# Uneven output products in one block, earlier weights' products, and another order at the start of batch 1, in a Fourier-mixing and gated-MLP kernel

## The chip, the cores and the metric

The kernel runs on one core of a Trainium2 chip. The metric is the device time of one execution in microseconds (us), lower is better. The core has five engines that run side by side and wait for each other through semaphores: TensorE (PE in the profile) multiplies matrices, VectorE (DVE), ScalarE (ACT) and GpSimd (POOL) work element by element, and SyncE (SP) issues most of the transfers. Each engine takes its instructions in the order in which the program lists them.

## The reference

The input `x` has 8 batches of 3008 rows of 256 numbers. It is Fourier transformed over the rows and over the columns, the real part is kept, and every row of the result goes through a gated two-layer network.

```python
X = np.fft.fft(x, axis=1)
X = np.fft.fft(X, axis=2)
x = X.real.reshape(B * S, D)                  # (24064, 256)
gate = np.maximum(x @ w_gate, 0.0)            # w_gate, w_val: 256 x 1536
val = x @ w_val
out = (gate * val) @ w_out                    # w_out: 1536 x 256
```

## The kernel before

The transform over the 256 columns is multiplied into the weights: `WA` and `WB` (index 0 for the gate, 1 for the value) are products of small cosine and sine tables `TA`, `TB` with the loaded weights, made in thirds of 512 columns by `weights` (L420). The first third is made at the start; `weights(1)` and `weights(2)` each give four steps, and each step is two matmuls into a bank of the pool `psO`, and a copy into `WA` or `WB` by ScalarE or VectorE.

The transform over the rows is made by matmuls with tables `tabC`, `tabS` (L585 in the profile). For each batch it gives `U` and `V`, with 1505 positions each. One position stands for two output rows that mirror each other: the first row's gate is a sum of products with `WA` and `WB`, and the other row's is reached by adding one more product with the negative doubled sine part (`mirror`, L880). The same holds for the value.

Batch 0 is worked in four blocks (`segments`) of 376 or 377 positions, the other batches in three blocks (`thirds`). A block has 12 tiles, one for each 128 of the 1536 hidden columns. In batch 0 a tile (`single_tile`, or `first_tile` in the first block) runs so: gate product of the first rows (two matmuls), relu on ScalarE into `r`; the mirror product of the tile before into its value bank `v`, and that tile's second `h` on VectorE; value product of this tile (two matmuls), first `h` (L899); a few output products; extra steps; mirror product into this tile's gate bank, second relu; a few more output products. The output products (L781, 256 columns each, `o<-wo,h`) belong to the block before, whose `h` are complete: they wait as a list, `todo_out`, from which `run` takes the next few. Two units of 128 rows share a bank of `psO`, and after 24 products a copy `os<-o` by ScalarE (L794) is put on the list `evict`. `run` ends with `flush`, which issues the copies on the lists, as long as tiles are not paired (that is in batch 0). Steps of the next batch's transform come from the list `todo_dft`, at counts given in tables such as `DFT_0`.

The third block is `blk == 2`. The second block's output products begin early, in its own last four tiles (24 of 72), so that 48 are left for the third block: `per_tile` is 4, and each tile took 2 and 2.

The dictionary `more` holds the extra steps by block and tile. In the first block there stand the eight steps of the weights (tiles 0 to 7), then the steps of the even tables; at tile 2 of the third block stands `gate_128`: it makes `b2`, 128 x 12 numbers, by turning row 0 of `WB[0]` with twelve matmuls of one column, and VectorE copies them out of the bank (L836, L837). `b2` is needed from batch 1 on.

From batch 1 on the order is that of `slot`. A tile's gate is split: `sine_part` makes the product with `V` in the only bank of `psG` (L1015), and ScalarE copies it out (L1018); `seed` has ScalarE write a scaled row `CB` times `b2` into a bank of `psP` (L1010), and `cosine_part` adds the product with `U` there (L1022); `both` forms the two gates on VectorE and GpSimd (L1026, L1027). While one tile (`cur`) is at its value product, the sine and cosine parts of the tile after next (`nxt`) are made, and the one behind that is seeded. The first tile of batch 1 has `lead` set. The last tile of batch 0 makes the first two tiles' parts in its steps `last`.

Of the kernel before, what the change touches and what calls it, by code (L numbers as in the profile page):

```python
# [11 lines left out]
F32 = mybir.dt.float32  # L12
# [17 lines left out]
def dram(ap, offset, pattern):  # L30
    return bass.AP(ap.tensor, offset, [list(p) for p in pattern])
# [3 lines left out]
def kernel(  # L35
# [27 lines left out]
    def single(name, shape, dt=F32, pool=const):  # L63
        return pool.tile(shape, dt, name=name, tag=name)
# [438 lines left out]
    start_pool.__exit__(None, None, None)  # L503
    ch128 = nc.dram_tensor("ch128", (B, 4 * NJ + 1), BF16, kind="Internal").ap()
    b2 = single("b2", [128, NF])
    one = single("one", [1, 1], BF16)
    nc.vector.memset(one[:], 1.0)


    def even_table(n, c):  # L510
# [311 lines left out]
    fold_even()  # L822
    turns_and_rows()

    more = {(0, i): [s] for i, s in enumerate(weights(1) + weights(2))}
    for n, c in enumerate(even_order):
        for k, step in enumerate(even_table(n, c)):
            more.setdefault(divmod(EVEN_AT[n] + k, NF), []).append(step)
# [1 line left out]
    for seg in (2, 3):  # L830
        more.setdefault((1, 8 + seg), []).append(lambda seg=seg: minus_v(nc.scalar, seg))

    def gate_128():
        p = psD.tile([128, 512], F32, name="d", tag="d")
        for f in range(NF):
            nc.tensor.matmul(p[:, f:f + 1], lhsT=WB[0][0:1, f * 128:(f + 1) * 128], rhs=one[:], start=True, stop=True)  # L836
        nc.vector.tensor_scalar(b2[:], p[:, 0:NF], scalar1=1.0, op0=ALU.mult, scalar2=None)  # L837
    more[(2, 2)] = [gate_128]
    more_1 = {}
    for at, step in zip((-5, -4, -3, -2, -1, 7, 7, 8, 14, 17), channel_loads() + channel_turn()):  # L840
        (more_1 if at >= 0 else more).setdefault(at if at >= 0 else (3, NF + at), []).append(step)

    DFT_0 = (0, 0, 0, 0, 0, 3, 0, 0, 4, 3, 3, 0), (0, 0, 0, 0, 0) + (1,) * 7, (3, 3, 3, 3, 3, 3, 0, 0, 0, 0, 0, 0)

    DFT_EVEN = (3, 0, 3, 0, 0, 0) * 4 + (0,) * 12
    DFT_1 = (3, 0, 3, 0, 0, 0) * 4 + (0, 1, 0, 1, 1) + (0,) * 7
# [4 lines left out]
    def run(todo, n):  # L851
        for _ in range(min(n, len(todo))):
            todo.pop(0)()
        if not paired:
            flush()
# [84 lines left out]
    def single_tile(st, outs, extra=(), last=(), tag="p"):  # L940

        gate(st, tag)
        if pending is not None:
            finish(pending)
        value(st)
        mult(st, 0)
        run(todo_out, outs)
        for step in extra:
            step()
        mirror(st["g"], st, 0)  # L950
        relu(st)
        run(todo_out, outs)
        for step in last:
            step()
        return st

    def first_tile(st, extra, outs):
# [47 lines left out]
    def seed(st, p=None):  # L1005

        if st is None or st["kind"] == "o":
            return
        st["p"] = p or bank("p")
        nc.scalar.activation(st["p"][:, 0:st["n"]], st["c"], ACTF.Copy, scale=b2[:, st["fi"]:st["fi"] + 1])  # L1010
# [18 lines left out]
    def slot(cur, mid, nxt, after, outs, fold_us):  # L1029

        stop = len(todo_out)

        def out(part):
            run(todo_out, len(todo_out) - stop + outs * part // 8)
        old = nxt is not None and nxt["kind"] == "o"
        new = nxt is not None and not old
        if old:
            gate(nxt)
        lead = cur["lead"]
        if lead:  # L1040
            out(5)
        if new and mid["kind"] != "o":
            sine_part(nxt)
        out(3 if not lead else 5)
        out(5)
        if new and mid["kind"] == "o":
            sine_part(nxt)
        if new:
            cosine_part(nxt)
        seed(after)  # L1050
        if pending is not None:
            mirror(pending["v"], pending, 1)
        if pending is not None:
            second(pending)
        value(cur)
        if cur["kind"] == "o":
            mult(cur, 0, cur["first"])
        else:
            relu_mult(cur, 0)
        if new:  # L1060
            both(nxt)
        if old:
            nxt["first"] = nxt["r"]
            mirror(nxt["g"], nxt, 0)
            relu(nxt)
        run_fold(fold_us)
        run_one(evict)
        run_one(sums)
        out(8)
        return cur  # L1070
# [4 lines left out]
    for b in range(B):  # L1075
# [4 lines left out]
        for blk, block in enumerate(blocks):  # L1080
# [53 lines left out]
            elif not paired:  # L1134
                for fi in range(NF):
                    st = tile_of(block, fi, (U, V, CB))
                    add_h(st, hs)
                    tag = {(3, 8): "g", (3, 9): "d", (3, 10): "g", (3, 11): "d"}.get((blk, fi), "p")
                    last = []
                    if (blk, fi) == (3, 11):  # L1140
                        last = [lambda: (sine_part(ahead[1]), cosine_part(ahead[1]), both(ahead[1]), seed(ahead[2]))]
                    if (blk, fi) == (3, 9):
                        ahead = [next(tiles) for _ in range(3)]
                        more[(3, 9)] += [lambda: seed(ahead[0], prime())]
                        more[(3, 10)] += [lambda: seed(ahead[1], prime())]
                        more[(3, 11)] += [lambda: (sine_part(ahead[0]), cosine_part(ahead[0]), both(ahead[0]))]
                    if (blk, fi) == (1, 8):
                        run(todo_out, len(todo_out))
                        todo_out = out_steps(b, block, hs, True)
                    pending = single_tile(st, 3 if blk == 1 else per_tile // 2, more_b.get((blk, fi), ()), last, tag)  # L1150
                    run(todo_dft, DFT_0[blk - 1][fi])
            else:
                for fi in range(NF):
# [59 lines left out]
```

## Time and profile before

| | |
|---|---|
| median of 3 runs | 631.07 us (631.01 to 631.09) |
| the profiled execution | 630.98 us |
| its span | 629.2 us, 12441 instructions |
| TensorE busy | 620.5 us (99%) |
| VectorE busy | 551.5 us (88%) |
| ScalarE busy | 445.5 us (71%) |
| GpSimd busy | 502.7 us (80%) |
| transfers | 66.47 MB, 106 GB/s on average |

The span is the time from the first to the last instruction of the profiled execution; its whole time is 1.8 us longer. A row of a timeline has the start in us from the start of the span, the duration in us, the engine, the line of the kernel, the operation with the tiles that it writes and reads, and the shape; `xN` merges N neighbours into one row, and a bracket at the end tells how long the engine was idle before and which instruction released it. A matmul's duration holds the passage through the array, so neighbours overlap; the distance of two starts is what one costs. Lines can be those of a helper: L781 is every output product.

### The profile page before, as it was taken

What the parts mean: (1) busy time and instruction counts of PE and PEld (TensorE: products, weight loads), DVE (VectorE), ACT (ScalarE), POOL (GpSimd) and SP (SyncE); (2) the same over time, 40 slices, a digit from 0 to 9 for tenths busy, and PEclk for the clock granted to TensorE, in tenths of its full rate; (3) what the DMA queues carried; (4) which work ended last, traced back from release to release, by engine and by line L of the source; (5) the groups of instructions that cost most, each with busy time, mean ns of one, the idle gap of its engine ahead of it and who ended that gap; (6) DMA issues with size and microseconds to landing.
All of it is one profiled execution on the core that took longest, in us unless ns stands there. A gap on an engine that the chain in (4) does not pass through costs nothing.

```text
span 629.2 us, 12441 instructions
## 1 busy us (share of the span) xinstructions
PE 620.5 (99%) x4114; PEld 398.4 (63%) x4114; DVE 551.5 (88%) x981; ACT 445.5 (71%) x813; POOL 502.7 (80%) x478
## 2 busy tenths in 40 slices
PE   8999999999999999999999999999999999999997
PEld 2566666566666666666666666666666666666666
DVE  8886676999899899988999999899999989999991
ACT  7796667777777767777777777777777777777762
POOL 8887992898999988799979989699886566666660
PEclk9999999999999999999999999999999999999999
DMA  9953748734264327315362426211221111211113
GB/s 240 209 206 118 173 177 102 182 73 151 82 150 145 126 76 183 113 44 165 83 187 64 140 76 130 68 50 36 77 61 38 42 60 56 57 38 51 51 44 102
DMA packets 82911, 66.47 MB, mean 106 GB/s; under 512 B 38517, under 2 KB 65941, under 8 KB 82846
## 3 DMA queue, kind: packets, MB, share of 16 engines
q1 hardware_dynamic: 78260, 60.01, 34.3%
q0 software_dynamic: 3984, 4.92, 3.9%
q10 hardware_dynamic: 602, 0.75, 0.4%
q8 instruction: 32, 0.52, 0.4%
q14 instruction: 33, 0.27, 0.2%
HBM read 41.88 MB, written 34.16 MB: 121 GB/s over the span
## 4 chain that ended last, share of the span: by engine, by line
PE 91%; DVE 4%; issue 2%; POOL 1%; DMA 1%; ACT 1%; DVEq 0%; ACTq 0%; POOLq 0%
PE o L781 36%; PE v L880 10%; PE v L875 9%; PE v L874 9%; PE g L1015 8%; PE p L1022 8%; PE d L585 4%; DVE h L910 2%; PE p L880 1%; PE p L874 1%; PE p L875 1%; DMA XG<-in_x_dram,gidx 1%; DVE h L899 1%; DVE r L1026 1%; POOL XG L120 1%
## 5 line engine op out<-in xcount | busy, mean ns | idle before, releaser
L1027 POOL TENSOR_TENSOR r<-r 128x512 f32<-128x512 f32 (+1 forms) x251 | 313.2, 1254 | 100.5 <-DVE r L1026 98.1
L910 DVE SCALAR_TENSOR_TENSOR h<-r,v 128x512 bf16<-128x512 f32 (+1 forms) x502 | 317.1, 673 | 39.2 <-PE v L880 26.5
L781 PE MATMUL o<-wo,h 128*128 128x256 bf16 x2172 | 330.6, 272 | 0.0
L781 PEld LDWEIGHTS <-h 128*128 128x128 bf16 x2220 | 216.7, 98 | 112.0 <-issue 1.3
L1010 ACT ACTIVATE p<-CB,b 128x512 f32<-128x512 bf16 (+1 forms) x251 | 171.8, 684 | 73.4 <-DVE r L1026 72.1
L1018 ACT COPY r<-g 128x512 f32<-128x512 f32 (+1 forms) x251 | 145.1, 578 | 66.5 <-PE g L1015 57.4
L1026 DVE SCALAR_TENSOR_TENSOR r<-r,p 128x512 f32<-128x512 f32 (+1 forms) x251 | 167.9, 669 | 0.9 <-ACT r L1018 0.9
L875 PE MATMUL v<-V,WB 128*128 128x512 bf16 (+3 forms) x296 | 108.6, 367 | 0.0
L874 PE MATMUL v<-U,WA 128*128 128x512 bf16 (+3 forms) x296 | 108.6, 367 | 0.0
L880 PE MATMUL v<-V,WM 128*128 128x512 bf16 (+1 forms) x252 | 94.4, 375 | 0.8 <-DVE h L910 0.4
L1015 PE MATMUL g<-V,WM 128*128 128x512 bf16 (+1 forms) x251 | 94.1, 375 | 0.5 <-ACT r L1018 0.4
L1022 PE MATMUL p<-U,WA 128*128 128x512 bf16 (+1 forms) x251 | 94.1, 375 | 0.2 <-ACT p L1010 0.2
L899 DVE TENSOR_TENSOR h<-r,v 128x376 bf16<-128x376 f32 (+2 forms) x90 | 46.2, 546 | 17.6 <-PE v L880 10.1
L874 PEld LDWEIGHTS <-WA 128*128 128x128 bf16 x348 | 33.9, 97 | 39.5 <-issue 10.4
L875 PEld LDWEIGHTS <-WB 128*128 128x128 bf16 x348 | 34.0, 98 | 34.3 <-DVE WB L431 0.6
L794 ACT COPY os<-o 128x512 f32<-128x512 f32 x92 | 52.6, 571 | 3.5 <-issue 3.0
L198 POOL TENSOR_TENSOR XG<-XG,XD 128x510 f32<-128x510 f32 x42 | 53.0, 1270 | 0.8 <-DMA XG<-xr 0.8
L890 ACT ACTIVATE r<-p 128x376 f32<-128x376 f32 (+1 forms) x80 | 38.0, 486 | 17.8 <-PE p L880 9.0
L206 POOL TENSOR_TENSOR AA<-XG 128x510 f32<-128x510 f32 x42 | 45.5, 1093 | 0.0
L1015 PEld LDWEIGHTS <-WM 128*128 128x128 bf16 x251 | 24.6, 98 | 5.7 <-issue 0.3
L1022 PEld LDWEIGHTS <-WA 128*128 128x128 bf16 x251 | 24.5, 98 | 3.7 <-issue 0.8
L880 PEld LDWEIGHTS <-WM 128*128 128x128 bf16 x253 | 24.8, 98 | 3.1
(186 smaller groups left out, 412.3 us busy)
## 6 DMA issues: line engine op xcount, KB each, us to landing
out_dram<-os SPq DMA_DIRECT2D x124, 128.0 KB
xr<-in_x_dram SPq DMA_DIRECT2D x12, 768.0 KB
XG<-xr SPq DMA_DIRECT2D x12, 768.0 KB
XD<-in_x_dram SPq DMA_DIRECT2D x15, 512.0 KB
out_dram<-os SPq DMA_DIRECT2D x35, 112.0 KB
XD<-in_x_dram SPq DMA_DIRECT2D x8, 448.0 KB
CB<-ch SPq DMA_DIRECT2D x7, 376.2 KB
out_dram<-os SPq DMA_DIRECT2D x13, 96.0 KB
```

What stands on the lines that cost most here:

```text
L198: e.tensor_tensor(XG[p, r, t, ::-1, 1:D], XG[p, r, t, ::-1, 1:D], XD[p, r, t, :, D - 1:0:-1], op=ALU.add)
L781: nc.tensor.matmul(st["p"][0:m, q, :], lhsT=lhs(f), rhs=wo[:, f, :], start=(f == 0 and not (early and q)), stop=(f == NF - 1), skip_group_ ...
L874: nc.tensor.matmul(bank[:, 0:st["n"]], lhsT=WA[i][:, st["f"]], rhs=st["us"], start=True, stop=False)
L875: nc.tensor.matmul(bank[:, 0:st["n"]], lhsT=WB[i][:, st["f"]], rhs=st["vs"], start=False, stop=True)
L880: nc.tensor.matmul(bank[:, 0:st["n"]], lhsT=W[i][:, st["f"]], rhs=v, start=False, stop=True, skip_group_check=True)
L910: nc.vector.scalar_tensor_tensor(half_h(st, sign), in0=st["s"][1 + sign][:, 0:n], scalar=0.0, in1=st["v"][:, 0:n], op0=ALU.max, op1=ALU.mult)
L1010: nc.scalar.activation(st["p"][:, 0:st["n"]], st["c"], ACTF.Copy, scale=b2[:, st["fi"]:st["fi"] + 1])
L1015: nc.tensor.matmul(st["g"][:, 0:n], lhsT=WM[0][:, st["f"]], rhs=st["vs"], start=True, stop=True)
L1018: nc.scalar.copy(q[:, 0:n], st["g"][:, 0:n])
L1022: nc.tensor.matmul(st["p"][:, 0:n], lhsT=WA[0][:, st["f"]], rhs=st["us"], start=False, stop=True, skip_group_check=True)
L1026: nc.vector.scalar_tensor_tensor(sp[:, 0:n], in0=q[:, 0:n], scalar=-0.5, in1=st["p"][:, 0:n], op0=ALU.mult, op1=ALU.add)
L1027: nc.gpsimd.tensor_tensor(sm[:, 0:n], sp[:, 0:n], q[:, 0:n], op=ALU.add)
```

## The change

- The four steps of `weights(2)` stand in tiles 3 to 6 of the first block, one tile earlier; tile 3 has two steps.
- `gate_128` and the tile `one` are gone. Row 0 of `WB[0]` is written to a DRAM row (`wrow`) at tile 1 of the second block, read back as 128 x 12 single numbers into `brow` at tile 4, and copied into `b2` by ScalarE at tile 2 of the third block.
- `single_tile` gets a count from `OUTS_0`. In the second and fourth block it is 6, as before. In the third block it is 5 for tiles 0 to 4, 4 for tiles 5 and 11, and 3 for tiles 6 to 10. The larger half is taken first.
- In `single_tile` the copies on the lists are issued after the steps `last` instead of before them. Only the last tile of batch 0 has such steps.
- In `slot`, in the tile with `lead`, the cosine part of `nxt` and the seed of the tile behind it come after the value product and the first `h` of this tile, and its output products are taken at eighths 4, 4, 5, 8 of its share of 6. For other tiles the order is the same.

```diff
-    one = single("one", [1, 1], BF16)
-    nc.vector.memset(one[:], 1.0)
+    wrow = nc.dram_tensor("wrow", (1, DF), BF16, kind="Internal").ap()
+    brow = single("brow", [128, NF], BF16)
...
-    more = {(0, i): [s] for i, s in enumerate(weights(1) + weights(2))}
+    more = {(0, i): [s] for i, s in enumerate(weights(1))}
+    for i, step in enumerate(weights(2)):
+        more.setdefault((0, 3 + i), []).append(step)
...
-    def gate_128():
-        p = psD.tile([128, 512], F32, name="d", tag="d")
-        for f in range(NF):
-            nc.tensor.matmul(p[:, f:f + 1], lhsT=WB[0][0:1, f * 128:(f + 1) * 128], rhs=one[:], start=True, stop=True)
-        nc.vector.tensor_scalar(b2[:], p[:, 0:NF], scalar1=1.0, op0=ALU.mult, scalar2=None)
-    more[(2, 2)] = [gate_128]
+    more[(1, 1)].append(lambda: nc.sync.dma_start(out=wrow, in_=WB[0][0:1, :]))
+    more[(1, 4)].append(lambda: nc.sync.dma_start(out=brow[:], in_=dram(wrow, 0, [[1, 128], [128, NF]]), allow_slow_non_contiguous=True))
+    more[(2, 2)] = [lambda: nc.scalar.copy(b2[:], brow[:])]
...
+    OUTS_0 = (6,) * 12, (5, 5, 5, 5, 5, 4, 3, 3, 3, 3, 3, 4), (6,) * 12
...
         mult(st, 0)
-        run(todo_out, outs)
+        run(todo_out, outs - outs // 2)
         for step in extra:
             step()
         mirror(st["g"], st, 0)
         relu(st)
-        run(todo_out, outs)
+        for _ in range(outs // 2):
+            run_one(todo_out)
         for step in last:
             step()
+        run(todo_out, 0)
         return st
...
         lead = cur["lead"]
-        if lead:
-            out(5)
+        out(4 if lead else 0)
         if new and mid["kind"] != "o":
             sine_part(nxt)
-        out(3 if not lead else 5)
-        out(5)
+        out(4 if lead else 5)
         if new and mid["kind"] == "o":
             sine_part(nxt)
-        if new:
+        if new and not lead:
             cosine_part(nxt)
-        seed(after)
+        if not lead:
+            seed(after)
         if pending is not None:
             mirror(pending["v"], pending, 1)
...
             relu_mult(cur, 0)
+        if lead:
+            out(5)
+            cosine_part(nxt)
+            seed(after)
         if new:
             both(nxt)
...
-                    pending = single_tile(st, 3 if blk == 1 else per_tile // 2, more_b.get((blk, fi), ()), last, tag)
+                    pending = single_tile(st, OUTS_0[blk - 1][fi], more_b.get((blk, fi), ()), last, tag)
```

## The prediction

> **What bounds the kernel now.** I read the busy table first, then the list of TensorE's waits, then the timelines of TensorE and ScalarE around each place that the diff touches, and the work of each stretch of the span.
>
> ```profile
> PE 620.5 (99%) x4114; PEld 398.4 (63%) x4114; DVE 551.5 (88%) x981; ACT 445.5 (71%) x813; POOL 502.7 (80%) x478
> PEclk9999999999999999999999999999999999999999
> ```
>
> TensorE is busy for 99% of the span at full clock, and from 107.87 us to the end for 517.07 of 521.33 us. So time comes out only where TensorE does less or stands still, and a microsecond won early moves everything behind it forward, unless that is tied to another engine or a transfer. The change touches three stretches, and TensorE's own rows there are what to read (start, duration, line, operation, and in brackets the idle time with its releaser).
>
> ```profile
> 30.10 0.32 PE L874 MATMUL d<-U,WA 128*128 128x376 bf16 x1
> 30.63 0.33 PE L875 MATMUL d<-V,WB 128*128 128x376 bf16 x1 [0.20 <-DVE WB L431]
> 30.80 0.49 PE L781 MATMUL o<-wo,h 128*128 128x256 bf16 x3
> ...
> 63.98 0.38 PE L781 MATMUL o<-wo,h 128*128 128x256 bf16 x2
> 64.29 0.45 PE L836 MATMUL d<-one,WB 1*128 1x1 bf16 x12
> 64.67 0.33 PE L880 MATMUL p<-CB,WB 128*128 128x376 bf16 x1
> ...
> 104.74 0.49 PE L781 MATMUL o<-wo,h 128*128 128x256 bf16 x3
> 105.66 0.38 PE L1015 MATMUL g<-V,WM 128*128 128x512 bf16 x1 [0.44 <-ACT r L1018]
> 106.25 0.38 PE L1022 MATMUL p<-U,WA 128*128 128x512 bf16 x1 [0.21 <-ACT p L1010]
> 106.47 0.32 PE L880 MATMUL v<-CB,WB 128*128 128x377 bf16 x1
> ```
>
> Successive starts without a wait lie 0.159 us apart for a 376-column product, 0.109 for a 256-column output product and 0.215 for a 512-column one; durations overlap. By starts the holes are 0.37 us before 30.63, 0.60 before 105.66 and 0.38 before 106.25.
>
> ScalarE, in order, shows why, and how an output copy (`os`) delays what is behind it:
>
> ```profile
> 51.14 0.48 ACT L890 ACTIVATE r<-p 128x376 f32<-128x376 f32 x1
> 51.52 0.58 ACT L794 COPY os<-o 128x512 f32<-128x512 f32 x1
> 51.99 0.50 ACT L890 ACTIVATE r<-p 128x376 f32<-128x376 f32 x1
> ...
> 104.15 0.49 ACT L890 ACTIVATE r<-d 128x377 f32<-128x377 f32 x1
> 104.53 0.59 ACT L794 COPY os<-o 128x512 f32<-128x512 f32 x1
> 105.00 0.62 ACT L1018 COPY r<-g 128x512 f32<-128x512 f32 x1
> 105.47 0.73 ACT L1010 ACTIVATE p<-CB,b 128x512 f32<-128x512 bf16 x1
> ```
>
> **Part 1, weights' products one tile earlier.** The four products of the last weight third (two 512-column matmuls each, 0.43 us by starts) move from tiles 4 to 7 of the first block to tiles 3 to 6. TensorE does the same work, so its start at tile 8 is the same (30.1). What changes is the copy of the last one into WB on VectorE: it now starts at 29.89, and the value product of tile 8 waits for it until 30.63. A tile earlier (1.4 us) it is done by about 29.6, and the product goes at 30.10 + 0.159 = 30.26: **0.37 us** less. Tile 3 then makes two weight products, so ScalarE copies twice in a row at 24.06 and 24.55; the next relu starts at 25.04 instead of 24.55, but TensorE gives its input 0.43 later too, and one copy less follows in tile 5, so this costs nothing. Cover that could fail: the output products start at 30.43 instead of 30.80, and they need `wo`, issued at 15.10 with 15.1 us to landing, so there at 30.2; 0.2 us are left. Ends: 0.15 (wo 0.2 later) and 0.41. I take 0.37.
>
> **Part 2, twelve small products out, one row through DRAM in.** L836's twelve matmuls run from 64.29 to 64.67, with 0.09 us of switch-over before: 0.47 us of TensorE, and 0.16 us on VectorE (L837), go. In come two transfers on SP's queue and a 128x12 copy on ScalarE. The write of the row waits for nothing new (WB is ready at 30.6) and goes when SP is idle, between 32.3 and 41.75. The read back, 1536 pieces of 2 bytes, comes behind the output store at 45.49, and SP has nothing more to issue until 52.13, so its issue (0.7 us, as the first CX load of 3072 pieces of 4 bytes took) costs nothing. Landing: that CX load took 5.5 us from issue by the packet records, the slowest row here, `wo`, 15.1: so between 51 and 61 us. The copy is due at 63.7 us, in tile 2 of the third block. Its cost is bounded by nothing and VectorE's like copy (0.16); ScalarE idles 0.41 before the relu behind it, so nothing is taken.
>
> **Part 3, the third block's spread.** 48 output products are left for its twelve tiles, before 4 in each, now 5 in tiles 0 to 4, 4 in tiles 5 and 11, 3 in tiles 6 to 10. I count from one L880 on `v` to the next; the first is at 60.54, the one after the last tile at 80.83: 20.29 us. The twelve periods before are 1.48, 1.48, 1.88, 1.48, 1.50, 2.59, 1.92, 1.54, 1.60, 1.64, 1.58, 1.60.
> A loop sets a floor: L880 on `v`, 0.43 to VectorE's start, two `h` products in 1.00, 0.05 back: 1.48. Without a transform step TensorE's work with 4 output products is 6 x 0.159 + 4 x 0.109 = 1.39, so it idled; with 5 it is 1.50. Tiles 0, 1, 2: 1.50 each, against 4.84 with the small products: 0.34 won, which holds part 2's 0.47.
> With one transform step, 4 output products make 1.55 plus a 0.04 wait for the relu; with 3 it is 1.44 + 0.04, at the floor. Tile 6 keeps 1.92 (VectorE's copy of N at 71.24 holds it). Tiles 7 to 10: 1.48, 1.48, 1.53, 1.49 instead of 6.36: 0.38 won.
> The loss: the output copies move. Before, the first followed tile 3's first relu (66.27), the second came under the 12 small-row products of tile 5 (69.83). Now the pairs end in the second run of tiles 2 and 4, and each copy comes right between a tile's second relu and the next one's first. The rows at 51 us show this order: L880 on `p` at 50.78, the next one at 52.54, 1.76 later = 0.36 to the relu + 0.38 + 0.48 (copy) + 0.48 (relu) + 0.05; around the copy at 80.71 it is 79.97 to 81.73, 1.76 again. For tile 3 (natural period 1.50) this is 0.25 lost, for tile 5 (two products in its first run, natural 1.39 to 1.43) 0.36 lost where 0.04 was. Tiles 3, 4, 5: 1.75, 1.50, 2.91 against 5.57: 0.59 lost.
> Sum of parts 2 and 3: 0.34 + 0.38 - 0.59 = **0.13 us**. Ends: 0.7 if the two copies cost nothing, -0.2 if the loop adds its wait behind them.
>
> **Part 4, batch 1's first products.** The last output copy of batch 0 (104.53) moves behind the steps of the last tile, and the third tile's cosine product and the fourth's seed behind the value product and first `h` of tile 0. Worked on from 104.31, with durations as above: the sine copy (L1018) starts at 104.72 (0.41 behind its product) instead of 105.00, ends at 105.33, and the next sine product goes at 105.37 instead of 105.66. Then L880 at 105.58 and the value products at 105.74 and 105.95 without a wait. The seed (L1010) runs from 105.20 to 105.93, so the cosine product at 106.17 does not wait. Three output and three transform products bring the next sine product to 107.19 instead of 107.87: **0.68 us**. The delayed output copy is at 105.83, the sine copy behind it ends at 106.9, in time. VectorE makes tile 0's `h` by 107.1, and L880 needs it at 107.95. Nothing of SP's queue waits more: it issues CX loads from 101.50 to 107.58. Ends: 0.3 (the first sine wait alone) and 0.98 (both holes).
>
> **Sum.** 0.37 + 0.13 + 0.68 = 1.18 us. The profiled execution took 630.98 us (span 629.22 and 1.76 around it), 0.09 below the median of 631.07; 630.98 - 1.18 = **629.8 us**. Work tied to other clocks is not reached: the CB row that the seeds read lands at 98.4 by the packet records, the first seed moves from 100.06 to 99.6; the reversed input of batch 3 lands at 119.5 and GpSimd takes it at 122.5, then 121.3. Behind 107.87 I change nothing.
>
> **Rivals.**
> A. The copies in the third block cost nothing: 1.18 + 0.57 = 1.75 won, 629.2 us. For it: VectorE idles 0.48 in each of these tiles, and TensorE works ahead of the loop; before, a copy in tile 3 cost only 0.12 (67.67). Against: the two places with the same order, 1.76 both times.
> B. One of the gains is given back: `wo` lands late (-0.2), VectorE's loop in batch 1 (1.28 + 0.68 of a 2.1 us slot) or the sine copy behind the moved output copy (0.48) turns into a new wait. 0.5 to 0.7 less: 630.4 us. For it: L880 on `v` has holes of 0.09 at 110.45 and 0.32 at 128.52 already.
> C, slower: the 2-byte read lands late. ScalarE then stands at the 128x12 copy in tile 2, all relus behind it, and TensorE half a tile later. From 63.7 us on each microsecond costs one; slower by 0.2% needs landing after 63.7 + 1.2 + 1.3 = 66.2, 20 us behind the issue: 632.5 us. Against it: the 15.1 us of `wo`, 256 times its bytes, is the longest here. For it: the queue was full once (issues of 8 us at 68.99 and 122.48), behind DRAM-to-DRAM loads that are not ahead of this one.
> The Trainium skill is on this rival's side (DMA: Bandwidth & Descriptors, Rules for kernel authors): a strided last dimension becomes one descriptor per element, and one should rearrange the data instead. The trace agrees that there is a packet for each element (over 2,400 packets of 4 bytes within 2 us at the CX loads), but at a median of 9 ns each. With the 10.5 ns a packet that the same page measured for GpSimd's loads (section Measured), an estimate for 1536 packets on 16 engines is 1.0 us, so that the sum would not move; by its rule taken as a warning the time is that of this rival, whose 0.08 rests on the rows above.
>
> **How the numbers follow.** A measurement tells about 0.2%, 1.26 us, from no change; the bound is 629.81. My forecast has 0.52, rival A 0.14, B 0.26, C 0.08. The forecast lies on the bound: half of it counts as faster, 0.26, with A 0.40; the other half and B make 0.52; C 0.08. The range takes in A, B and the ends of the terms: 1.18 less 0.2, 0.3 and 0.4 on one side (630.7, and 0.3 more for a new hole in batch 1 like that at 128.52: 631.0), plus 0.57 and 0.3 on the other (628.9).
>
> **What would show it.** Right: no wait before d<-V,WB near 30.2; no L836, a 128x12 copy on ScalarE with no idle time ahead; L880 on `p` with holes of 0.25 and 0.35 in tiles 3 and 5 of the third block, v-to-v total near 20.16; the sine product of the third tile 0.3 us behind the outputs and no wait on its cosine. Wrong: a DMA as releaser on ScalarE near 63 us, a wait for `wo` at 30.4, or new holes after 107.

## The result, and the profile after

| | before | after |
|---|---|---|
| median | 631.04 us (630.84 to 631.25, 22 runs) | 630.15 us (629.76 to 630.80, 22 runs) |
| the profiled execution | 630.98 us | 630.04 us |
| its span | 629.2 us, 12441 instructions | 628.3 us, 12374 instructions |

The ratio is 0.9986, with a 95% interval of 0.9981 to 0.9992: about 0.9 us faster. That is less than the 0.2% that the prediction took as the least a measurement can tell, but the interval does not reach 1. The forecast was 629.8 us (628.9 to 631.0), so the time lies in the range, and 0.3 of the 1.18 us did not come.

First the page of the kernel after: the span, the busy table and the granted clock.

```profile
span 628.3 us, 12374 instructions
PE 617.2 (98%) x4057; PEld 397.6 (63%) x4102; DVE 550.7 (88%) x979; ACT 445.5 (71%) x814; POOL 502.2 (80%) x478
PEclk9999999999999999999999999999999999999999
```

TensorE is the bound as before, at full clock. Its busy time isn't to be compared with before: 45 weight loads have no matmul record beside them in this trace, so matmul records are missing.

TensorE's timeline of the kernel after, at the places shown of before (start, duration, line, operation; in brackets the idle time and its releaser):

```profile
30.14 0.32 PE L875 MATMUL d<-U,WA 128*128 128x376 bf16 x1
30.30 0.32 PE L876 MATMUL d<-V,WB 128*128 128x376 bf16 x1
30.45 0.49 PE L781 MATMUL o<-wo,h 128*128 128x256 bf16 x3
...
65.17 0.49 PE L781 MATMUL o<-wo,h 128*128 128x256 bf16 x3
65.76 0.32 PE L881 MATMUL p<-CB,WB 128*128 128x376 bf16 x1
...
66.29 0.32 PE L876 MATMUL p<-V,WB 128*128 128x376 bf16 x1
66.54 0.32 PE L881 MATMUL v<-CB,WB 128*128 128x376 bf16 x1
...
68.52 0.38 PE L781 MATMUL o<-wo,h 128*128 128x256 bf16 x2
69.10 0.32 PE L881 MATMUL p<-CB,WB 128*128 128x376 bf16 x1 [0.20 <-ACT r L891]
...
104.42 0.49 PE L781 MATMUL o<-wo,h 128*128 128x256 bf16 x3
105.04 0.38 PE L1018 MATMUL g<-V,WM 128*128 128x512 bf16 x1
...
105.85 0.38 PE L1025 MATMUL p<-U,WA 128*128 128x512 bf16 x1
...
106.87 0.38 PE L1018 MATMUL g<-V,WM 128*128 128x512 bf16 x1
```

Read by starts. The value product of tile 8 now follows its neighbour at the natural 0.159 us, and the output products follow without a wait for `wo`. In the third block there are holes before L881 on `p`: 65.17 + 3 x 0.109 = 65.50, but it goes at 65.76 (0.26), and 68.52 + 0.22 = 68.74, but it goes at 69.10 (0.37). L881 on `v` at 66.54 is another 0.09 late. Before the third sine product 0.30 is left of 0.60, and the cosine product has no wait.

Counted between the same places of both traces, the 0.94 us of span come from here. The first output product is 0.35 earlier (30.80, then 30.45). From there to the third block's first L880 or L881 on `v` nothing changes (29.74 in both). The third block takes 20.32 us instead of 20.29. Then 22.43 in both to batch 1's first sine product, 3.93 instead of 4.61 from that to the fourth one, and 521.40 instead of 521.35 to the end. So parts 1 and 4 are there in full, and parts 2 and 3 together gave nothing. Tile by tile, in us:

| third block, tile | 0 | 1 | 2 | 3 | 4 | 5 | 6 | 7 | 8 | 9 | 10 | 11 | sum |
|---|---|---|---|---|---|---|---|---|---|---|---|---|---|
| before | 1.48 | 1.48 | 1.88 | 1.48 | 1.50 | 2.59 | 1.91 | 1.55 | 1.59 | 1.64 | 1.59 | 1.60 | 20.29 |
| forecast | 1.50 | 1.50 | 1.50 | 1.75 | 1.50 | 2.91 | 1.92 | 1.48 | 1.48 | 1.53 | 1.49 | 1.60 | 20.16 |
| after | 1.50 | 1.50 | 1.50 | 1.85 | 1.50 | 2.92 | 1.91 | 1.48 | 1.48 | 1.60 | 1.48 | 1.59 | 20.32 |

Two tiles miss the forecast: tile 3 by 0.10 and tile 9 by 0.07. ScalarE's timeline of the kernel after shows the copy of `b2`, the output copy in tile 3, the other copy (`es`) in tile 9, and the start of batch 1.

```profile
62.86 1.08 ACT L891 ACTIVATE r<-p 128x376 f32<-128x376 f32 x2 [0.42 <-PE p L881]
63.83 0.19 ACT L837 CAST b<-brow 128x12 f32<-128x12 bf16 x1
64.36 0.48 ACT L891 ACTIVATE r<-p 128x376 f32<-128x376 f32 x1 [0.33 <-PE p L881]
64.74 0.58 ACT L794 COPY os<-o 128x512 f32<-128x512 f32 x1
65.20 0.50 ACT L891 ACTIVATE r<-p 128x376 f32<-128x376 f32 x1
...
75.41 0.48 ACT L891 ACTIVATE r<-p 128x376 f32<-128x376 f32 x1 [0.41 <-PE p L881]
75.78 0.47 ACT L592 COPY es<-d 128x376 f32<-128x376 f32 x1
76.14 0.50 ACT L891 ACTIVATE r<-p 128x376 f32<-128x376 f32 x1
...
104.41 0.58 ACT L1021 COPY r<-g 128x512 f32<-128x512 f32 x1
104.89 0.70 ACT L1013 ACTIVATE p<-CB,b 128x512 f32<-128x512 bf16 x1
105.51 0.59 ACT L794 COPY os<-o 128x512 f32<-128x512 f32 x1
```

The copy of `b2` runs between two relus with no transfer as its releaser, and the relu behind it waits for TensorE, not for the copy. The output copy at 64.74 stands between one tile's second relu (64.36) and the next one's first (65.20), and `es` at 75.78 stands in the same place. The first relu of a tile must have read its bank before L881 on `p` may add to it, so this delay reaches TensorE. The gate product of 64.53 ended at 64.85, but its relu starts only at 65.20, behind the copy. That ScalarE's queue is strictly in order is also what the Trainium skill says (TensorE: Matmul & The Clock Gate, Architectural detail: the array is 16× 32×32, not 1× 128×128), and these rows agree. The forecast had counted the output copies and not `es`. The tile that reads `brow`, in the kernel after:

```profile
L836 SPq DMA_DIRECT2D brow<-wrow x1: 509/509/509, 46.3 to 46.3; - x1
L837 ACT CAST b<-brow x1: 192/192/192, 63.8 to 63.8; 128x12 f32<-128x12 bf16 x1
```

Its issue took 0.51 us. By the packet records 1536 packets ran from 48.10 to 50.11 us, and the last of the sixteen updates of its semaphore came at 51.37, 12.5 us ahead of its use.

VectorE's timeline holds the 0.10 that the forecast lacked in tile 3. Before:

```profile
63.93 1.00 DVE L899 TENSOR_TENSOR h<-r,v 128x376 bf16<-128x376 f32 x2 [0.48 <-PE v L880]
64.85 0.16 DVE L837 TENSOR_SCALAR b<-d 128x12 f32<-128x12 f32 x1
65.80 1.00 DVE L899 TENSOR_TENSOR h<-r,v 128x376 bf16<-128x376 f32 x2 [0.80 <-PE v L880]
```

and after:

```profile
63.62 1.00 DVE L900 TENSOR_TENSOR h<-r,v 128x376 bf16<-128x376 f32 x2 [0.50 <-PE v L881]
65.49 1.00 DVE L900 TENSOR_TENSOR h<-r,v 128x376 bf16<-128x376 f32 x2 [0.86 <-PE v L876]
```

The pair at 65.49 needs only the mirror product on `v` of 64.69. The trace records VectorE's waits for a semaphore as instructions of their own, and the wait for this product ends at 65.08. In the other tiles a pair starts 0.045 us behind the end of that wait; here it is 0.41. The value product in the bracket (L876) is merely the last thing that TensorE had signalled. The relu that its first `h` reads had begun at 64.36 and was done by 64.84. No wait in the program accounts for the rest.

### The profile page after: what moved, and what is told of

Same layout as the page of the kernel before. It is cut to its first block, busy times and chain, and to the rows that moved or that the text cites. A ratio compares the mean times of both kernels' runs of the same rounds, so it can differ in the third digit from the quotient of the medians.

```text
span 628.3 us, 12374 instructions
## 1 busy us (share of the span) xinstructions
PE 617.2 (98%) x4057; PEld 397.6 (63%) x4102; DVE 550.7 (88%) x979; ACT 445.5 (71%) x814; POOL 502.2 (80%) x478
## 4 chain that ended last, share of the span: by engine, by line
PE 91%; DVE 4%; issue 2%; POOL 1%; DMA 1%; ACT 1%; DVEq 0%; POOLq 0%; ACTq 0%
PE o L781 36%; PE v L876 10%; PE v L881 10%; PE g L1018 8%; PE p L1025 8%; PE v L875 8%; PE d L585 4%; DVE h L911 2%; PE p L881 1%; PE p L875 1%; PE p L876 1%; DMA XG<-in_x_dram,gidx 1%; DVE r L1029 1%; PE o L427 1%; POOL XG L120 1%
## 5 line engine op out<-in xcount | busy, mean ns | idle before, releaser
L876 PE MATMUL v<-V,WB 128*128 128x512 bf16 (+3 forms) x296 | 108.7, 367 | 2.2
L881 PE MATMUL v<-V,WM 128*128 128x512 bf16 (+1 forms) x252 | 94.4, 375 | 1.1 <-DVE h L911 0.7
L875 PE MATMUL v<-U,WA 128*128 128x512 bf16 (+3 forms) x254 | 92.8, 365 | 0.0
L876 PEld LDWEIGHTS <-WB 128*128 128x128 bf16 x348 | 33.9, 97 | 33.6 <-ACT WB L677 0.2
L881 PEld LDWEIGHTS <-WM 128*128 128x128 bf16 x253 | 24.7, 98 | 3.1
```

Source lines behind the costliest of these rows:

```text
L875: nc.tensor.matmul(bank[:, 0:st["n"]], lhsT=WA[i][:, st["f"]], rhs=st["us"], start=True, stop=False)
L876: nc.tensor.matmul(bank[:, 0:st["n"]], lhsT=WB[i][:, st["f"]], rhs=st["vs"], start=False, stop=True)
L881: nc.tensor.matmul(bank[:, 0:st["n"]], lhsT=W[i][:, st["f"]], rhs=v, start=False, stop=True, skip_group_check=True)
```

## The experiments

All medians are beside runs of the kernel before in the same set. These gave 631.04 us for the first four, 631.08 for the next four and 631.18 for the last four. "Block" is the third block, counted as above; 20.29 before.

| | median (lowest to highest) | ratio to before, 95% | block |
|---|---|---|---|
| x1: part 1 alone | 630.67 (630.33 to 631.04) | 0.9994 [0.9985, 1.0003] | 20.29 |
| x2: part 2 alone | 630.77 (630.48 to 630.99) | 0.9996 [0.9987, 1.0005] | 20.20 |
| x3: part 3 alone | 631.42 (631.23 to 631.58) | 1.0007 [0.9998, 1.0016] | 20.71 |
| x4: part 4 alone | 630.08 (629.96 to 630.40) | 0.9986 [0.9977, 0.9995] | 20.29 |
| y1: x2 and the memset | 630.64 (630.45 to 630.80) | 0.9994 [0.9985, 1.0003] | 19.90 |
| y2: after and the memset | 629.81 (629.57 to 629.93) | 0.9979 [0.9970, 0.9988] | 20.22 |
| x5: after, 4 each | 629.93 (629.72 to 630.05) | 0.9981 [0.9972, 0.9990] | 20.21 |
| x6: after, copies moved | 629.29 (629.09 to 629.96) | 0.9974 [0.9963, 0.9984] | 19.99 |
| x7: x6, 4 each | 629.54 (629.39 to 630.18) | 0.9975 [0.9965, 0.9986] | 20.21 |
| x8: half of part 4 | 630.86 (630.53 to 631.13) | 0.9995 [0.9986, 1.0004] | 20.30 |
| x9: other half of part 4 | 630.48 (630.13 to 630.91) | 0.9990 [0.9981, 0.9999] | 20.30 |
| y3: x6 and the memset | 628.97 (628.92 to 629.18) | 0.9966 [0.9952, 0.9979] | 19.64 |

The start of one and the same program differs between executions: in the seven profiled executions that keep the weights' old order, the first output product is at 30.52 to 30.96 us. So single parts are judged by their own stretch of the trace, and the medians, which also hold this spread, stand beside it.

### Each part alone (x1 to x4)

x1, on the kernel before:

```diff
-    more = {(0, i): [s] for i, s in enumerate(weights(1) + weights(2))}
+    more = {(0, i): [s] for i, s in enumerate(weights(1))}
+    for i, step in enumerate(weights(2)):
+        more.setdefault((0, 3 + i), []).append(step)
```

> Part 1 alone: the weights' products of the last third one tile earlier, all else as before. Theory (each part acts in its own place and the gains add): the wait of 0.37 us on d<-V,WB near 30.6 is gone and all behind it is 0.33 earlier, as in the changed kernel: 630.7 us. Rival (given back downstream, by ScalarE's table work at 39 to 46 us, which is full): the wait goes, but the holes before L880 on p near 42.6 and 44.5 (0.38 and 0.15) grow by the same, 631.0 us.

The wait before the value product of tile 8 is gone: it starts 0.16 us behind its neighbour instead of 0.53. This repeats in every profile: all seven with the old order have a hole of 0.37 there, all seven with the new order none. From the first block's mirror product on `v` at 21.09 (in the kernel before) to the first output product the seven with the old order take 9.71 us and the seven with the new one 9.30 (9.29 in two), so part 1 is worth 0.41 us. The median, 0.37 less, agrees, though its interval reaches past 1.

x2, on the kernel before: the row goes through DRAM, and `one`, its memset, the twelve products and VectorE's copy are gone.

```diff
-    one = single("one", [1, 1], BF16)
-    nc.vector.memset(one[:], 1.0)
+    wrow = nc.dram_tensor("wrow", (1, DF), BF16, kind="Internal").ap()
+    brow = single("brow", [128, NF], BF16)
...
-    more[(2, 2)] = [gate_128]
+    more[(1, 1)].append(lambda: nc.sync.dma_start(out=wrow, in_=WB[0][0:1, :]))
+    more[(1, 4)].append(lambda: nc.sync.dma_start(out=brow[:], in_=dram(wrow, 0, [[1, 128], [128, NF]]), allow_slow_non_contiguous=True))
+    more[(2, 2)] = [lambda: nc.scalar.copy(b2[:], brow[:])]
```

> Part 2 alone: the twelve small products are replaced by the row through DRAM, the output products stay 4 in each tile of the third block. Theory: tile 2 of the third block goes from 1.88 to its floor of 1.48 us, 0.40 less: 630.6 us; the copy of b2 on ScalarE waits for no transfer. Rival (the small products filled time in which the loop over VectorE would have held TensorE anyway): tile 2 keeps most of its 1.88, 631.0 us.

The block takes 20.20, only 0.09 less. Tile 2 fell from 1.88 to 1.48 as it should, but tile 3 rose from 1.48 to 1.85. TensorE's timeline of x2 there:

```profile
65.94 0.32 PE L872 MATMUL p<-V,WB 128*128 128x376 bf16 x1
66.55 0.32 PE L877 MATMUL v<-CB,WB 128*128 128x376 bf16 x1 [0.29 <-DVE h L896]
```

and VectorE's, of the same kernel:

```profile
63.65 1.00 DVE L896 TENSOR_TENSOR h<-r,v 128x376 bf16<-128x376 f32 x2 [0.48 <-PE v L877]
65.50 1.00 DVE L896 TENSOR_TENSOR h<-r,v 128x376 bf16<-128x376 f32 x2 [0.84 <-PE v L872]
```

TensorE waits for an `h` that VectorE began late, with the same late start as in the kernel after and with no output copy near. So neither the spread nor the copies make it. The place in VectorE's own program was left as a cause: the instruction is VectorE's record number 191 of the trace, with its semaphore waits counted too, from 0. Looked through for it, the traces show such late starts, 0.40 to 0.41 us behind the end of the wait just ahead, at records whose numbers differ by multiples of 128: 319 (119.30 us) and 575 (220.75 us) in the kernel before, 191 (65.49) and 447 (170.28) in the kernel after. In the kernel before, record 191 is the copy of `b2`, for which nothing waits. The change takes two instructions out of VectorE's program ahead of this place, so another instruction stands there.

x3, on the kernel before (the small products and their memset stay):

```diff
+    OUTS_0 = (6,) * 12, (5, 5, 5, 5, 5, 4, 3, 3, 3, 3, 3, 4), (6,) * 12
...
-        run(todo_out, outs)
+        run(todo_out, outs - outs // 2)
...
-        run(todo_out, outs)
+        run(todo_out, outs // 2)
...
-                    pending = single_tile(st, 3 if blk == 1 else per_tile // 2, more_b.get((blk, fi), ()), last, tag)
+                    pending = single_tile(st, OUTS_0[blk - 1][fi], more_b.get((blk, fi), ()), last, tag)
```

> Part 3 alone: output products 5, 5, 5, 5, 5, 4, 3, 3, 3, 3, 3, 4 in the third block, the twelve small products still there. Theory (an output copy between a tile's second relu and the next one's first costs 0.25 to 0.36 us): the third block takes 20.3 + 0.47 = 20.8 us instead of 20.29, so that the spread by itself is a loss: 631.5 us. Rival A of the prediction (the copies cost nothing): 20.2 us and 631.0 us or less.

The block gets 0.42 longer: 1.50, 1.50, 1.99, 1.76, 1.50, 2.92, 1.91, 1.48, 1.48, 1.60, 1.48, 1.59. Tile 3 is 1.76 here, the forecast's 1.75, and tile 5 is 2.92, the forecast's 2.91. So the price of an output copy between two relus of the loop is right, and without the late start tile 3 has no more than that. The spread by itself costs time; the fall of tiles 7 to 10 (6.04 instead of 6.37) doesn't pay for it.

x4, on the kernel before: the two edits in `single_tile` that issue the copies behind `last`, and the new order in `slot` (both are shown at x8 and x9).

> Part 4 alone: the last output copy of batch 0 behind the steps of its last tile, and in the first tile of batch 1 the cosine product and seed behind the value product. Theory: 104.31 to 107.87 shrinks by 0.68, 630.4 us. Rival B of the prediction (new waits behind it take back about half): 630.7 us, with new holes between 107 and 135 us.

From the first to the fourth sine product it takes 3.93 instead of 4.61, the forecast's 0.68. The median says 0.96. The rest isn't in this stretch: the profiled execution also began 0.15 earlier, as starts differ, and was 0.19 shorter from the fourth sine product to the end. That second difference comes from the late starts. The new order gives VectorE one more semaphore wait at the start of batch 1, so the records numbered by 128 are other instructions from there on: the holes of 0.24 and 0.23 us that TensorE has before the mirror products at 222.09 and 566.31 in the kernel before are gone in x4, and one of 0.22 at 320.34 has come. In the kernel after, where two other instructions are gone as well, they lie elsewhere again, and the time to the end is 521.40 against 521.35.

The parts' blocks don't add up to the whole: -0.09 and +0.42 against +0.03. In tile 3 the late start (+0.37 in x2) and the copy (+0.28 in x3) fall together, and the kernel after pays 0.37 once (1.85 against 1.48).

### A memset that nothing reads (y1, y2)

If the place in VectorE's program is the cause, one more instruction far ahead must cure it. Both kernels put the memset of `one` back, which nothing reads any more: y1 in x2, y2 in the kernel after.

```diff
+    one = single("one", [1, 1], BF16)
+    nc.vector.memset(one[:], 1.0)
```

> Part 2 alone, as in x2_row, but the small VectorE memset of the tile one stays near the start of VectorE's program, so that all that follows stands one instruction later in it. In x2_row tile 3 of the third block took 1.85 us because one h on VectorE started 0.43 us after its semaphore event with nothing to wait for. Theory P (every 128th record of VectorE's program starts about 0.4 us late, and the removed instructions moved such a place onto this h): the late start moves away, tile 3 goes back to 1.48 us, and the third block takes 19.83 instead of 20.20: 630.4 us. Rival (the copy of b2 on ScalarE holds that h up): tile 3 stays at 1.85 us, 630.8 us.

> The changed kernel with the memset put back as the only difference. Theory P: tile 3 of the third block goes from 1.85 to 1.75 us (the hole before L881 on v behind the output copy goes, the one before L881 on p stays), and the late start that fell on an h at 170.3 us moves too: 0.1 to 0.3 less, 629.9 to 630.05 us. Rival (b2's copy): no change, 630.15 us.

In y1 tile 3 is back at 1.48 and the block at 19.90, 0.39 less than before. VectorE's timeline of y1:

```profile
63.97 1.00 DVE L898 TENSOR_TENSOR h<-r,v 128x376 bf16<-128x376 f32 x2 [0.48 <-PE v L879]
65.46 1.00 DVE L898 TENSOR_TENSOR h<-r,v 128x376 bf16<-128x376 f32 x2 [0.48 <-PE v L879]
```

The idle time of 0.84 ahead of the second pair is 0.48 again. In y2 tile 3 is 1.75 and the block 20.22: the 0.10 that the forecast lacked there. By the median the added instruction gains 0.34 us in y2 against the kernel after. In y1 it is 0.13 against x2, with intervals that overlap, and the 630.4 us that Theory P forecast was missed: the third block won 0.30 us, but from the fourth sine product to the end y1 takes 521.47 instead of 521.22, since the late starts behind it have moved too. What in the chip does this every 128 records isn't shown by these runs (the last section has what the traces show beside it). The times here come from executions with a recorded span, so it is also open whether it would happen without a recording.

### The output copies and the spread (x6, x5, x7)

x6, on the kernel after: the copies on the lists are issued at the first run of a tile only, that is between its own two relus, and behind the steps for batch 1.

```diff
     def run(todo, n):
         for _ in range(min(n, len(todo))):
             todo.pop(0)()
-        if not paired:
+        if n and not paired:
             flush()
...
-        run(todo_out, 0)
+        if last:
+            flush()
```

> The changed kernel with the copies on the lists not issued at the end of a tile of batch 0 when nothing is to be run there, so that an output copy ending a tile comes behind the first relu of the next one. Theory (an output copy between two relus holds TensorE for 0.25 to 0.36 us): the holes before L881 on p in tiles 3 and 5 of the third block (0.26 and 0.37), in the second block (0.15 twice) and at the start of the fourth (0.10) go or shrink to a few hundredths; the third block takes 19.8 instead of 20.3: 629.2 us. Rival (the floor of VectorE's loop takes the time instead): the holes reappear before L881 on v, 629.9 us or more.

The block takes 19.99, 0.33 less. Tile 5 is 2.59 as before the change. TensorE's timeline of x6 at the two places:

```profile
65.51 0.32 PE L876 MATMUL p<-V,WB 128*128 128x376 bf16 x1
66.02 0.32 PE L881 MATMUL v<-CB,WB 128*128 128x376 bf16 x1 [0.18 <-DVE h L900]
...
68.00 0.38 PE L781 MATMUL o<-wo,h 128*128 128x256 bf16 x2
68.25 0.32 PE L881 MATMUL p<-CB,WB 128*128 128x376 bf16 x1
```

and ScalarE's of the same kernel, which shows the new order:

```profile
67.18 1.02 ACT L891 ACTIVATE r<-p 128x376 f32<-128x376 f32 x2 [0.82 <-PE p L881]
68.10 0.58 ACT L794 COPY os<-o 128x512 f32<-128x512 f32 x1
68.61 0.48 ACT L891 ACTIVATE r<-p 128x376 f32<-128x376 f32 x1
```

The copy now stands between a tile's first relu and its second, where ScalarE idles for TensorE anyway. The relu at 68.61 starts 0.36 behind L881 on `p` (68.25), as without a copy, and that L881 has no wait. Tile 3 is still 1.85, now from the late start alone. The second block gains too: from the first output product to the third block's start it is 29.50 instead of 29.74, since two holes of 0.15 of the same kind, which the kernel before has as well, are gone.

x5, on the kernel after, has `(4,) * 12` for the third block; x7 is x6 with the same.

```diff
-    OUTS_0 = (6,) * 12, (5, 5, 5, 5, 5, 4, 3, 3, 3, 3, 3, 4), (6,) * 12
+    OUTS_0 = (6,) * 12, (4,) * 12, (6,) * 12
```

> The changed kernel with 4 output products in each tile of the third block, so parts 1, 2 and 4 without the spread. Theory, with the late start of VectorE in tile 3 still there: third block 20.2 us as in x2_row instead of 20.32, 630.0 us. If the spread by itself cost what x3_spread showed (0.43), it would be 629.7 us.

> x6_late with 4 output products in every tile of the third block instead of 5,5,5,5,5,4,3,3,3,3,3,4. If the spread gains by itself once the copies lie well (0.38 in tiles 7 to 10, since 3 products leave these tiles at the floor of VectorE's loop): tiles 7 to 10 take 1.55, 1.59, 1.64, 1.59 as before instead of 1.48, 1.60, 1.48, 1.59, tiles 0 to 4 keep 1.48, so the block gets 0.2 to 0.35 longer than x6_late's 19.99 and the kernel takes 629.5 to 629.6. Rival (the spread only moves idle time about): the block stays within 0.1 of 19.99, and the time at 629.3.

x5 has 20.21, 0.11 less than the uneven spread; tile 3 is 1.84 from the late start, tile 5 is 2.55, and tiles 7 to 10 are as before the change. x7 has 20.21 too, 0.22 more than x6. So the sign of the spread turns on where the copies lie. In the kernel as it is, the uneven spread brings them between one tile's second relu and the next one's first, and it costs 0.11 (x5 to after). With the copies out of the way it gains 0.22 (x7 to x6): tiles 7 to 10 are 6.04 instead of 6.38, less the 0.11 by which tiles 0, 1, 2, 4 and 5 are longer. The 0.11 of cost is small only because the late start holds tile 3 in both x5 and the kernel after: without it, from y1 with 4 each to y2 with the uneven spread (they differ in parts 1 and 4 too, outside the block), the block goes from 19.90 to 20.22, a cost of 0.32.

### Part 4 in halves (x8, x9)

x8, on the kernel before, only puts the copy behind the steps for batch 1:

```diff
-        run(todo_out, outs)
+        for _ in range(outs):
+            run_one(todo_out)
         for step in last:
             step()
+        run(todo_out, 0)
```

> Half of part 4 alone on the kernel before: in the last tile of batch 0 the output copy comes behind the steps for batch 1 instead of ahead of them; the order of the first tile of batch 1 is as before. If the two waits are separate terms: the sine copy starts at 0.41 behind its product, the hole before the third sine product shrinks from 0.60 to 0.30, the cosine product still waits for its seed (a hole of 0.3 to 0.4), and from the first sine product of batch 1 to the fourth it takes 4.33 instead of 4.61; 630.75 us. Rival (both waits have one cause, the output copy, which holds the sine copy and the seed behind it): both holes shrink, 4.33 to 3.95, 630.4.

x9, on the kernel before, is only the order in `slot`:

```diff
-        if lead:
-            out(5)
+        out(4 if lead else 0)
...
-        out(3 if not lead else 5)
-        out(5)
+        out(4 if lead else 5)
...
-        if new:
+        if new and not lead:
             cosine_part(nxt)
-        seed(after)
+        if not lead:
+            seed(after)
...
+        if lead:
+            out(5)
+            cosine_part(nxt)
+            seed(after)
```

> The other half of part 4 alone on the kernel before: the cosine product of the third tile, the seed of the fourth and the last output products come behind the value product and the first `h` of the first tile of batch 1; the output copy stays ahead of the steps. If the two waits are separate terms: the hole of 0.60 before the third sine product stays, the one of 0.38 before the cosine product goes, since the value products fill it, and from the first sine product to the fourth it takes 4.23 instead of 4.61; 630.65 us. Rival (the wait for the seed only moves to the next user of ScalarE): a new hole before the fourth sine product or the mirror product, 4.5 to 4.6, 631.0.

TensorE's timeline of x8:

```profile
104.88 0.49 PE L781 MATMUL o<-wo,h 128*128 128x256 bf16 x3
105.50 0.38 PE L1017 MATMUL g<-V,WM 128*128 128x512 bf16 x1
106.09 0.38 PE L1024 MATMUL p<-U,WA 128*128 128x512 bf16 x1 [0.22 <-ACT p L1012]
```

and of x9:

```profile
104.91 0.49 PE L781 MATMUL o<-wo,h 128*128 128x256 bf16 x3
105.84 0.38 PE L1015 MATMUL g<-V,WM 128*128 128x512 bf16 x1 [0.44 <-ACT r L1018]
```

x8 halves the first hole (0.30 instead of 0.60) and keeps the second (0.38); the stretch takes 4.31, 0.30 less. x9 keeps the first (0.60) and fills the second; 4.24, 0.37 less. (Its median, 0.70 less, also holds 0.18 behind this stretch: like x4 it has one more VectorE wait, and the same hole of 0.22 near 320 us in place of the two of the kernel before.) The two add up to 0.67, and part 4 as a whole has 0.68. So these are two separate waits and not one with the output copy as its cause.

### Both repairs (y3)

x6 with the memset put back, as in y1.

> The changed kernel with both repairs: the lists of output copies are issued only at the first run of a tile and, in the tile with the steps of batch 1, behind them (as in x6_late), and the memset of `one` is put back, although nothing reads it, so that VectorE's 191st record falls on another instruction (as in y2_after_memset). Theory P (every 128th record of VectorE starts 0.4 us late, and it costs time only where TensorE stands behind that instruction): tile 3 of the third block goes back from 1.85 to 1.50, the block from 19.99 to about 19.65, and the kernel takes 0.35 us less than x6_late, 628.9. Rival (tile 3 of x6_late is long because its two copies meet there, whatever VectorE's records do): tile 3 stays at 1.85, the block at 19.99 and the time at 629.3.

The block takes 19.64, with tiles 0 to 4 at 1.50 each. The median is 628.97 us, 0.9966 of before, the fastest of all here. TensorE's timeline of y3 at tile 3, where x6 waits:

```profile
65.83 0.32 PE L878 MATMUL p<-V,WB 128*128 128x376 bf16 x1
65.99 0.32 PE L883 MATMUL v<-CB,WB 128*128 128x376 bf16 x1
```

By stretches its span is 2.01 us shorter than before: 0.31 at the start, 0.24 in the second block, 0.65 in the third, 0.15 in the fourth, 0.68 at the start of batch 1, and nothing after that.

## Why the prediction came out as it did

**Part 1: right.** 0.37 was taken; the hole was 0.37 and the stretch around it got 0.41 shorter, seven profiles against seven. Between the two profiled executions it is 0.35, since the start itself differs. `wo` was not late at the output products: they follow the value product by 0.16 us.

**Part 2: right for TensorE, incomplete for VectorE.** With the late start out of the way (y1) it is worth 0.39, close to 0.47 less the 0.09 by which VectorE's loop of 1.48 holds tile 2 anyway. The transfer landed 5.1 us behind its issue, where the nearest like row (the CX load) gave 5.5. The copy on ScalarE cost nothing, as taken. What the working left out is what else the two removed VectorE instructions do. It costed their removal at nothing or a gain, and named no row for a loss. It moved a late start of 0.41 us from an instruction that nobody waited for to one that TensorE waits for. That isn't to be had from durations; but a VectorE start far behind its wait stood in the trace of before, at 119.30 and 220.75.

**Part 3: the mechanism right, the sum short.** The output copies cost 0.26 in tile 3 (1.76 in x3, 1.50 without in y3) and 0.33 in tile 5 (2.92 and 2.59); forecast were 0.25 and 0.32. Tiles 7 to 10 were to fall by 0.38 and fell by 0.33 by the trace: tile 9 was put at 1.53 and is 1.60. Its `es` copy (75.78) stands between two tiles' relus, just as the output copies do, and leaves a hole of 0.17 ahead of L881 on `p`. The rule that the prediction used for the output copies of tiles 3 and 5 had not been used on this copy.

**The term that was mis-sized** is thus the 0.13 for parts 2 and 3 together. It measured -0.03: 0.10 from the late start in tile 3 and 0.07 in tile 9. It lay within its ends of 0.7 and -0.2. With 0.02 at the start and 0.06 behind batch 1's start, that is the difference between the 1.18 forecast and the 0.94 by which the profiled executions differ. The medians differ by 0.89.

**Part 4: right in each step.** 0.68 forecast, 0.68 measured; the sine product 0.30 behind the outputs, no wait on the cosine product, and the two waits separate (x8, x9). What it does besides, moving VectorE's late starts in the batches behind it by one more wait (x4), was not in the working.

**The rivals.** A (the copies cost nothing) falls with x3 and x6: they cost about 0.3 each, and moving them gains it back. C (the row's read lands late) falls with the landing at 51.4 us for a use at 63.8. The Trainium skill's warning (DMA: Bandwidth & Descriptors, Rules for kernel authors: one descriptor for each element of a strided last dimension) does describe what was done, 1536 packets for 1536 numbers, at a median of 9 ns; at this size, and landed 12.5 us ahead of its use, it cost nothing. The prediction's estimate of 1.0 us for these packets was worked out wrongly: the Trainium skill's 10.5 ns a packet (DMA: Bandwidth & Descriptors, Measured) is the elapsed time of a whole small transfer over its 64 packets, and the prediction divided it by 16 engines once more. Undivided, the estimate is 16 us and would have weighed for rival C. The packets here took 2.0 us in all. B (a gain is given back, 630.4) is nearer to the median in time than the forecast is, 0.25 against 0.35 us. But its places do not show it: there was no wait for `wo`, and the sine copy was in time. TensorE's waits for VectorE behind the start of batch 1 only changed place with the late starts: 0.24 and 0.23 us (222.09 and 566.31) before, 0.21 at 171.56 and 0.37 more at 615.60 after, which is 0.06 in the time to the end. Most of what was lost, 0.16 us, was lost in the third block, in part by a cause that none of the rivals had.

## What to carry to other kernels

On an engine that takes its work in order, look between which two operations a copy falls: ahead of an operation that the bound engine soon waits for it is part of that loop, in an idle place it is free. Count this for each copy in the stretch, and not only for those that the change moves. A spread of filler work can't be judged without it: the same uneven spread cost 0.11 us here with the copies in the wrong place (0.32 where no late start hid it) and gained 0.22 with them in the right one. And where an engine starts late without any wait, note the instruction's number in that engine's program: adding or removing an instruction far ahead moves that delay onto another instruction, and a change can lose or gain by that alone.

## What the runs showed of the hardware

VectorE's records, its semaphore waits counted too and numbered from 0, show a late start every 128 records: 191, 319, 447, 575 and so on. In the fourteen traces, 40 instructions with such a number stand directly behind a wait that ended while VectorE was idle, and all 40 started 0.40 to 0.42 us behind the end of that wait. For the 2860 other instructions in this position the median is 0.045 us. Only seven of them took more than 0.2: the same `h` at 42 us in the seven kernels with the new order of the weights, which waits for a relu as well. Where VectorE is busy or still waits at such a record, nothing shows.

It costs time only where TensorE stands behind the late instruction: 0.37 us in tile 3 of the third block in x2. Another place is the mirror product on `v` behind VectorE's start at 220.75 in the kernel before. There it is 0.46 us behind its neighbour:

```profile
221.63 0.38 PE L1022 MATMUL p<-U,WA 128*128 128x512 bf16 x1
222.09 0.38 PE L880 MATMUL v<-V,WM 128*128 128x512 bf16 x1
```

and in the kernel after, whose late starts lie on other instructions, the usual 0.21:

```profile
220.85 0.38 PE L1025 MATMUL p<-U,WA 128*128 128x512 bf16 x1
221.06 0.38 PE L881 MATMUL v<-V,WM 128*128 128x512 bf16 x1
```

One memset of a single element that nothing reads moved the late start away from tile 3, and the medians fell by 0.3 us (after to y2, x6 to y3).

The page of the kernel after lists, among the queues, transfers of a kind named `instruction` (packets, MB, share); those of this queue have 8192 bytes each:

```profile
q14 instruction: 33, 0.27, 0.1%
```

Behind 38 of the 40 late starts one of them begins 0.65 to 1.45 us later. So the loading of the engine's program is a likely cause, but no run varies it, and the cause stays open.
